# The low rank term's second product: from 32-row float32 tiles to one 128-row float32r product

## Chip, cores and metric

One core of one Trainium2 chip runs the whole kernel. The metric is the device time of one execution in microseconds (us). All arrays are float32 in memory; the kernel's large products run in float32r, on operands that were first split into a rounded high part and a low part that holds the rest.

## The reference, cut to what matters

```python
x = attention(q, k, v)                 # windowed, 4 batches x 8 heads, 576 tokens, 64 wide
xt = x.transpose(0, 2, 1)              # [4, 512, 576]
h = xt @ U @ V                         # U [576, 32], V [32, 576]: the low rank term
u = x + h.transpose(0, 2, 1)
x = u + relu(u @ w_ch1) @ w_ch2        # 512 -> 2048 -> 512
...                                    
```

A gated block with LayerNorm and a 576x576 spatial product follows and gives the output [4, 576, 512]; the change does not touch it. The term in question is small: per batch `xt @ U` gives a [512, 32] matrix, which is then multiplied by V.

## The kernel before, in words

The kernel does not call the engines directly. Every piece of work is handed to a planner (class `Plan`) by `P.add(engine, cost, emit, r=..., w=..., prio=...)`, with a cost in us, the buffers that it reads and writes, and a priority. The planner places the tasks engine by engine in eight passes of a list schedule and emits the instructions in that order, so a change in a few tasks can reorder all the others. Some tasks may go to one of two engines: a PSUM copy by `copy(engines("t", ...))` to ACT (line 416) or DVE (line 417), the scaling of the attention weights to POOL (line 1080) or DVE (line 1082), a `minus` to DVE (line 602) or POOL (line 603).

The first 190 us are the attention. Its work runs over 4 batches x 4 pairs of heads: scores on PE (line 1044), bias and row maximum on DVE (line 1055), exponent on ACT (line 1060), scaling (1080, 1082), transposes on PE (line 1090), the product with v (line 1128). Between these, PE does the first products of the hidden layer for the batches that are done (lines 545 to 547 and 584 to 586, each three matmuls of 128x512: a "trio" below). After each batch come the tokens' transposes (line 1155) and the low rank term:

- `mix` (line 1171): for each pair of heads, U as a 32-column stationary operand against the transposed x, five chunks, float32. The four pairs write the four strips of 32 partitions of one PSUM tile `t`. Batch 0 does it in two halves of two pairs each, the other batches in one.
- One ACT copy of `t` to the SBUF tile `th` (line 416, `th<-at`).
- `up` (line 1184), for each half of 288 tokens: one float32 matmul for each pair, whose contraction is over the pair's own strip of 32 rows, with `th` as stationary and `v32` (V, copied four times, once onto each strip) as moving operand. All products of a half are one task and take as many PSUM buffers at once. A float32 product has two records in the trace.
- An add on DVE for each product into the attention's output `u` (line 1189).

`low_rank_weights` loads U and V, decodes them on ACT and DVE (lines 452 to 465), and copies V from `v4` to the strips of `v32` by four DMAs (line 983). SP issues all DMAs in the planner's order, one behind another, and an issue that waits for its data holds those behind it. PSUM buffers come from the rings `sc` and `at` (three each, four in batch 0).

Of the kernel before, what the change touches and what calls it, by code (L numbers as in the profile page):

```python
# [338 lines left out]
def tile_kernel(ctx, tc, qT, kT, v, U, V, w1, w2, w_in, wspT, bsp, w_out, bias, out):  # L339
    nc = tc.nc  # L340
# [82 lines left out]
    def engines(kind, usual):  # L423
        return BOTH if kind in K["flex"] else (usual,)
# [512 lines left out]
    def constant(name, shape, dtype):  # L937
        return Ring(in_att, name, 1).new(shape, dtype)
# [25 lines left out]
    for p in ps:  # L964
        for t in (0, 8):
            P.add("POOL", 0.1, lambda p=p, t=t: nc.gpsimd.memset(p[:, REST[t] * 128 + 64 : REST[t] * 128 + 128], 0.0),
                  w=[p.part("zero")], prio=-1)
    r_xt, r_th = Ring(in_att, "xt", 2), Ring(in_att, "th", 2)


    u32 = constant("u32", [128, 5, RANK], F32)
    v32 = constant("v32", [128, S], F32)

    def low_rank_weights(prio, early, prio_v, early_v):
        single(u32, [(0, block(U, 0, 128, 0, RANK)), (1, block(U, 64, S, 0, RANK, 4))], 5, RANK, prio, None, early)
        P.add("DVE", 0.1, lambda: nc.vector.memset(u32[64:, 0], 0.0), w=[u32], prio=prio)
        n = S // 2
        v4 = constant("v4", [128, 1, n], F32)
        single(v4, [(0, block(V, 0, RANK, i // 2 * n, i // 2 * n + n), slice(RANK * i, RANK * i + RANK)) for i in range(4)],
               1, n, prio_v, None, early_v)  # L980
        for q in range(2):
            for d in range(2):
                P.dma(64, n, lambda q=q, d=d: nc.sync.dma_start(
                    out=v32[64 * d : 64 * d + 64, q * n : q * n + n], in_=v4[64 * q : 64 * q + 64, 0]),
                    r=[v4], w=[v32.part((q, d))], prio=K["vc"])

    vl = {}
    spare = r_f1.new([128, 128], F32)
# [173 lines left out]
    def low_rank(b, xts, pairs, p0):  # L1162

        sc, tp = (r_sc0, r_at0) if b == 0 else (r_sc, r_at)
        rows = slice(pairs[0] * 32, pairs[-1] * 32 + 32)
        t, th = tp.new([128, 128], F32), r_th.new([128, 128], F32)

        def mix():
            for c in range(5):
                for pair in pairs:  # L1170
                    nc.tensor.matmul(t[pair * 32 : pair * 32 + 32], u32[:, c], xts[pair // 2][:, c, pair % 2],
                                     start=c == 0, stop=c == 4, skip_group_check=True)

        P.add("PE", 5 * 4 * 128 / 2400 + 0.1, mix, r=[u32] + [xts[h].part(c) for h in {p // 2 for p in pairs} for c in (0, 2, 4)],
              w=[t], prio=p0, mode="quarters")
        copy(engines("t", "ACT"), 128, lambda: th[rows], lambda: t[rows], PSUM, r=[t], w=[th], prio=p0 + 0.05)
        for s0 in (0, 288):
            sl = slice(s0, s0 + 288)
            outs = [(sc, tp)[pair % 2].new([128, 288], F32) for pair in pairs]

            def up(sl=sl, outs=outs):
                for pair, o in zip(pairs, outs):
                    d = slice(pair * 32, pair * 32 + 32)
                    nc.tensor.matmul(o.ap(), th[d], v32[d, sl], start=True, stop=True)

            P.add("PE", 4 * 288 / 2400 + 0.1, up, r=[th] + list(v32.parts.values()), w=outs, prio=p0 + 0.1, mode="quarter rows")
            for pair, o in zip(pairs, outs):
                ub = u[b][pair]
                P.add("DVE", dve(288), lambda o=o, ub=ub, sl=sl: nc.vector.tensor_tensor(
                    out=ub[:, sl], in0=o.ap(), in1=ub[:, sl], op=ALU.add),  # L1190
                    r=[o], w=[ub.part(0), ub.part(1), ub], prio=p0 + 0.2)
# [544 lines left out]
```

## Time and profile before

| | us |
|---|---|
| median of the three runs | 714.19 |
| the runs | 713.57, 714.19, 2403.31 |
| the profiled execution, its own time | 713.79 |
| its span, first to last instruction | 712.0 |
| mean granted TensorE clock, of full speed | 1.000 |

The span is the time between the first and the last instruction; 1.8 us of the execution lie outside it. Busy time of an engine is the time in which at least one of its instructions ran. PE's matmuls overlap, so their starts tell more than their durations: the distance from one start to the next is what one of them costs in a full queue.

### The profile page before, as it was taken

How to read it: one execution, taken by the hardware profiler on the slowest of the kernel's cores; microseconds unless marked ns; L12 is line 12 of the kernel's file. 1: busy time of each engine (PE TensorE's matmuls, PEld its weight loads, DVE VectorE, ACT ScalarE, POOL GpSimd, SP SyncE). 2: the span in 40 equal slices, each digit the busy share in tenths (PEclk: the TensorE clock that was granted, in tenths of full speed). 3: DMA queues.
4: the chain of work that ended last, by engine and by line, in shares of the span. 5: the costliest groups of instructions: out<-in, count | busy, mean ns of one | idle time of the engine just before them, and what ended most of it. 6: DMA issues, size and time to landing. Idle time of an engine off the chain costs nothing.

```text
span 712.0 us, 14829 instructions
## 1 busy us (share of the span) xinstructions
PE 701.7 (99%) x5434; PEld 637.8 (90%) x5434; DVE 576.0 (81%) x1637; ACT 394.0 (55%) x1082; POOL 75.0 (11%) x114
## 2 busy tenths in 40 slices
PE   8989999999999999999999999999999999999998
PEld 6767778778799999999999999999998898898896
DVE  6999996775597999999695998696589989859561
ACT  7878666564353655547253562544267566566352
POOL 2243330310400000000000000040010100100000
DMA  8865212210074166628475555447694202100102
GB/s 233 280 221 161 66 52 82 72 53 2 1 225 157 42 228 220 223 106 267 149 225 175 168 195 185 144 148 264 239 386 174 80 30 68 54 22 0 60 1 75
DMA packets 58799, 98.48 MB, mean 138 GB/s; under 512 B 8357, under 2 KB 38309, under 8 KB 58726
## 3 DMA queue, kind: packets, MB, share of 16 engines
q1 hardware_dynamic: 58437, 97.23, 41.2%
q8 instruction: 43, 0.70, 0.4%
q14 instruction: 31, 0.25, 0.1%
q10 hardware_dynamic: 288, 0.30, 0.1%
HBM read 67.67 MB, written 29.54 MB: 137 GB/s over the span
## 4 chain that ended last, share of the span: by engine, by line
PE 88%; DVE 7%; ACT 2%; DMA 1%; issue 1%; POOL 0%; SPq 0%; POOLq 0%; ACTq 0%
PE sc L586 8%; PE sc L584 8%; PE sc L585 8%; PE at L885 6%; PE at L886 6%; PE at L887 6%; PE at L1128 3%; PE sc L1044 2%; PE sc L1423 2%; PE sc L1421 2%; PE sc L1422 2%; PE at L1090 2%; PE at L1423 2%; PE at L1421 2%; PE at L1422 2%; PE acc L584 2%
## 5 line engine op out<-in xcount | busy, mean ns | idle before, releaser
L584 PE MATMUL sc<-h,wa 128*128 128x384 f32 (+1 forms) x328 | 110.6, 337 | 0.0
L585 PE MATMUL sc<-h,wa 128*128 128x384 f32 (+1 forms) x328 | 110.5, 337 | 0.0
L586 PE MATMUL sc<-hl,wa 128*128 128x384 f32 x320 | 108.7, 340 | 0.0
L1060 ACT ACTIVATE p<-p,nmax 128x192 f32<-128x192 f32 (+2 forms) x144 | 61.5, 431 | 10.2 <-DVE nmax L1055 10.0
L584 PEld LDWEIGHTS sc<-h,wa 128*128 128x128 f32 x328 | 61.6, 188 | 0.3
L585 PEld LDWEIGHTS sc<-h,wa 128*128 128x128 f32 x328 | 61.5, 187 | 0.3
L933 DVE TENSOR_TENSOR y<-sc,y 128x384 f32<-128x384 f32 (+1 forms) x96 | 40.7, 450 | 25.6 <-PE sc L586 25.3
L885 PE MATMUL at<-xd,wa 128*128 128x384 f32 x180 | 60.9, 338 | 0.0
L886 PE MATMUL at<-xd,wa 128*128 128x384 f32 x180 | 60.8, 338 | 0.0
L887 PE MATMUL at<-xd,wa 128*128 128x384 f32 x180 | 60.8, 338 | 0.0
L586 PEld LDWEIGHTS sc<-hl,wa 128*128 128x128 f32 x320 | 60.1, 188 | 0.0
L1055 DVE CUSTOM_DVE_ANT_0 p<-sc,bias 128x192 f32<-128x192 f32 (+2 forms) x144 | 40.3, 328 | 12.7 <-PE sc L1044 12.4
L905 ACT COPY c<-at 128x384 f32<-128x384 f32 x54 | 25.8, 478 | 39.2 <-PE at L887 38.9
L416 ACT CAST wa<-st 128x256 fp32r<-128x256 f32 (+1 forms) x62 | 28.1, 475 | 25.2 <-DVE st L465 13.1
L897 ACT ACTIVATE h<-c 128x384 fp32r<-128x384 f32 x54 | 28.4, 526 | 19.7 <-DVE c L892 19.5
L892 DVE TENSOR_TENSOR c<-at,c 128x384 f32<-128x384 f32 x54 | 29.8, 551 | 8.2 <-PE at L887 4.9
L885 PEld LDWEIGHTS at<-xd,wa 128*128 128x128 f32 x180 | 33.8, 188 | 0.0
L886 PEld LDWEIGHTS at<-xd,wa 128*128 128x128 f32 x180 | 33.8, 188 | 0.0
L887 PEld LDWEIGHTS at<-xd,wa 128*128 128x128 f32 x180 | 33.8, 188 | 0.0
L1044 PE MATMUL sc<-kr,qr 64*64 64x192 f32 (+2 forms) x576 | 31.7, 319 | 1.2 <-DMA qr<-in_qT 0.7
L1090 PE MATMUL at<-ident,p 128*128 128x128 f32 x208 | 31.1, 281 | 1.5 <-DVE p L1082 1.4
L1090 PEld LDWEIGHTS at<-ident,p 128*128 128x128 f32 x208 | 23.0, 140 | 10.4 <-issue 3.3
(407 smaller groups left out, 2007.7 us busy)
## 6 DMA issues: line engine op xcount, KB each, us to landing
wa<-in_w SPq DMA_DIRECT2D x32, 512.0 KB, 4.3
xd<-formsa SPq DMA_DIRECT2D x24, 192.0 KB, 3.0
qr<-in_qT SPq DMA_DIRECT2D x15, 288.0 KB, 3.3
kr<-in_kT SPq DMA_DIRECT2D x15, 288.0 KB, 4.0
vr<-in_v SPq DMA_DIRECT2D x16, 256.0 KB, 4.3
raw<-in_w_in SPq DMA_DIRECT2D x8, 512.0 KB, 3.9
kepts<-raw SPq DMA_DIRECT2D x14, 288.0 KB, 2.1
out<-h SPq DMA_DIRECT2D x15, 256.0 KB, 2.0
```

The costliest lines, as they stand in the source:

```text
L584: nc.tensor.matmul(o, wt[:, 0, 0, c], hh[:, j], start=i == 0 and x == 0, stop=False, skip_group_check=True)
L585: nc.tensor.matmul(o, wt[:, 1, 0, c], hh[:, j], start=False, stop=False, skip_group_check=True)
L586: nc.tensor.matmul(o, wt[:, 0, 0, c], hl[:, j], start=False, stop=i == len(wts) - 1, skip_group_check=True)
L885: nc.tensor.matmul(o.ap(), wh()[:, k], xh.ap(), start=start and k == 0, stop=False, skip_group_check=True)
L886: nc.tensor.matmul(o.ap(), wl()[:, k], xh.ap(), start=False, stop=False, skip_group_check=True)
L887: nc.tensor.matmul(o.ap(), wh()[:, k], xl.ap(), start=False, stop=k == 1, skip_group_check=True)
L892: P.add("DVE", dve(N3), lambda: nc.vector.tensor_tensor(out=out.ap(), in0=ps_.ap(), in1=sb.ap(), op=ALU.add), r=[ps_, sb], w=[out], prio=0)
L933: P.add("DVE", dve(m), lambda acc=acc, dst=dst, s=s, m=m, o=o: nc.vector.tensor_tensor(out=dst[:, s : s + m], in0=acc[:, 0, o : o + m], in ...
L1044: nc.tensor.matmul(s[o : o + 64, c0 : c0 + k1 - k0], qr[d, 64 * t : 64 * t + 64], kr[d, k0:k1], start=True, stop=True, skip_group_check=True)
L1055: nc.vector.tensor_tensor_reduce(out=o(), in0=s[:, c0 : c0 + nk], in1=bias_t[:, pair, t % 2, 192 - nk :], scale=-0.125, scalar=BIG, op0=AL ...
L1060: nc.scalar.activation(out=o(), in_=o(), func=AF.Exp, scale=-1.0, bias=nmax[:, sl, t : t + 1], accum_out=sums[:, sl, t : t + 1])
L1090: P.add("PE", 0.109, lambda pt=pt, n_=n_, s0=s0: nc.tensor.transpose(pt[:, n_ - s0], p[:, n_ * 128 : n_ * 128 + 128], ident), r=[p.part(t) ...
```

## The change

The 32-row products become products over all 128 rows, in float32r. For each pair a zeroed tile `four[:, pair]` takes, on strips of 32 rows, the high part of `t`, its low part, and the high part again; the fourth strip stays zero. `v32` takes V's high part on the strips that stand against the first two and V's low part on the others. One product then sums high x high, low x high and high x low. (For pairs 2 and 3, whose strips of `t` are the lower ones, the strips are placed the other way round.) Each product is a task of its own with one PSUM buffer. `t` to `four` takes three operations for each pair: a copy (ACT or DVE), a subtraction (DVE), a copy (ACT or DVE). V gets a copy (ACT) and a subtraction (DVE) more before its four DMAs, and POOL a memset of `four` at the start.

```diff
-    r_xt, r_th = Ring(in_att, "xt", 2), Ring(in_att, "th", 2)
+    r_xt, four = Ring(in_att, "xt", 2), constant("four", [128, 4, 128], F32R)
+    P.add("POOL", 0.3, lambda: nc.gpsimd.memset(f32(four.ap()), 0.0), w=[four.part(pair) for pair in range(4)], prio=-1)
...
-    v32 = constant("v32", [128, S], F32)
+    v32 = constant("v32", [128, S], F32R)
...
-        v4 = constant("v4", [128, 1, n], F32)
+        v4, v4h = constant("v4", [128, 1, n], F32), Ring(in_left, "y", 0, more=["y_4"]).new([128, n], F32R)
...
+        P.add("ACT", act(n, 0.09), lambda: nc.scalar.copy(out=v4h.ap(), in_=v4[:, 0]), r=[v4], w=[v4h], prio=K["vc"])
+        minus(("DVE",), n, lambda: v4[:, 0].bitcast(F32R), lambda: v4[:, 0], lambda: f32(v4h.ap()), r=[v4h], w=[v4], prio=K["vc"])
         for q in range(2):
-            for d in range(2):
-                P.dma(64, n, lambda q=q, d=d: nc.sync.dma_start(
-                    out=v32[64 * d : 64 * d + 64, q * n : q * n + n], in_=v4[64 * q : 64 * q + 64, 0]),
-                    r=[v4], w=[v32.part((q, d))], prio=K["vc"])
+            for d, (src, t) in enumerate(((lambda: f32(v4h.ap()), v4h), (lambda: v4[:, 0], v4))):
+                P.dma(64, n, lambda q=q, d=d, src=src: nc.sync.dma_start(
+                    out=f32(v32[64 * d : 64 * d + 64, q * n : q * n + n]), in_=src()[64 * q : 64 * q + 64]),
+                    r=[t], w=[v32.part((q, d))], prio=K["vc"])
...
-        copy(engines("t", "ACT"), 128, lambda: th[rows], lambda: t[rows], PSUM, r=[t], w=[th], prio=p0 + 0.05)
+        strip = lambda g: slice(32 * g, 32 * g + 32)
+        for pair in pairs:
+            part, low = four.part(pair), 0 if pair == 1 else 1
+            copy(engines("t", "ACT"), 128, lambda pair=pair: four[strip(pair), pair], lambda pair=pair: t[strip(pair)], PSUM, r=[t], w=[part], prio=p0 + 0.05)
+            P.add("DVE", dve(128), lambda pair=pair, low=low: nc.vector.tensor_tensor(
+                out=four[strip(low), pair], in0=t[strip(pair)], in1=f32(four[strip(pair), pair]), op=ALU.subtract), r=[t], w=[part], prio=p0 + 0.05)
+            copy(engines("t", "ACT"), 128, lambda pair=pair: four[strip(2 if pair < 2 else 0), pair], lambda pair=pair: t[strip(pair)], PSUM, r=[t], w=[part], prio=p0 + 0.05)
         for s0 in (0, 288):
             sl = slice(s0, s0 + 288)
-            outs = [(sc, tp)[pair % 2].new([128, 288], F32) for pair in pairs]
-
-            def up(sl=sl, outs=outs):
-                for pair, o in zip(pairs, outs):
-                    d = slice(pair * 32, pair * 32 + 32)
-                    nc.tensor.matmul(o.ap(), th[d], v32[d, sl], start=True, stop=True)
-
-            P.add("PE", 4 * 288 / 2400 + 0.1, up, r=[th] + list(v32.parts.values()), w=outs, prio=p0 + 0.1, mode="quarter rows")
-            for pair, o in zip(pairs, outs):
-                ub = u[b][pair]
+            for pair in pairs:
+                o, ub = (sc, tp)[pair % 2].new([128, 288], F32), u[b][pair]
+                P.add("PE", mm(288), lambda pair=pair, o=o, sl=sl: nc.tensor.matmul(o.ap(), four[:, pair], v32[:, sl], start=True, stop=True),
+                      r=[four.part(pair)] + list(v32.parts.values()), w=[o], prio=p0 + 0.1)
```

In the order of instructions, 32 products stand in place of 32; 16 subtractions and 18 of the 32 copies are on DVE, 14 copies on ACT, where 5 copies (`th`) were. Of the scalings of attention weights DVE has 81 in place of 87, and of its other copies out of PSUM (line 417) 47 in place of 52. Lines of the attention have a number two or three higher in the changed kernel.

The first place is PE at the low rank term of the last batch (`xt` transposed x, `u_419` and `u_443` U, `v_441` and `v_471` the tile v32). Before:

```order
L1171 MATMUL at<-xt,u_419 32x128 x20
L584 MATMUL acc<-h,wa 128x512
L585 MATMUL acc<-h,wa 128x512
L586 MATMUL acc<-h,wa 128x512
L1184 MATMUL sc<-v_441,th 128x288
L1184 MATMUL at<-v_441,th 128x288
L1184 MATMUL sc<-v_441,th 128x288
L1184 MATMUL at<-v_441,th 128x288
L584 MATMUL acc<-h,wa 128x512
```

In the changed kernel the same place on PE reads:

```order
L1173 MATMUL at<-xt,u_443 32x128 x20
L584 MATMUL acc<-h,wa 128x512
L585 MATMUL acc<-h,wa 128x512
L586 MATMUL acc<-h,wa 128x512
L1189 MATMUL sc<-v_471,four 128x288 x2
L1189 MATMUL at<-v_471,four 128x288
L1189 MATMUL sc<-v_471,four 128x288
L1189 MATMUL at<-v_471,four 128x288 x2
L584 MATMUL acc<-h,wa 128x512
```

One trio stands between `mix` and the first products in both; behind it six products follow in place of four, and the last two stand two trios later.

The second place is DVE in the last batch, from the transposed tokens to the adds. Before, nothing of the low rank term stood between them:

```order
L417 COPY u<-at 128x4x64
L417 COPY xt<-at 128x512
L552 SCALAR_TENSOR_TENSOR h<-f_2822,h 128x512
L594 TENSOR_TENSOR y<-acc,u 128x128
L594 TENSOR_TENSOR y<-acc,u 128x384
L1189 TENSOR_TENSOR u<-sc,u 128x288
```

In the changed kernel DVE has there:

```order
L417 COPY u<-at 128x4x64
L417 COPY xt<-at 128x512
L552 SCALAR_TENSOR_TENSOR h<-f_2839,h 128x512
L417 CAST four<-at 32x128 x2
L1182 TENSOR_TENSOR four<-at,four 32x128 x2
L417 CAST four<-at 32x128 x2
L1182 TENSOR_TENSOR four<-at,four 32x128 x2
L594 TENSOR_TENSOR y<-acc,u 128x128
```

Eight operations on strips were put in, four more copies to `four` are on ACT.

The third place is DVE in the second half of batch 0 (`st` weights that are decoded, `p_77` attention weights). Before:

```order
L417 COPY xt<-at 128x512
L1068 RECIPROCAL rinv<-rinv 128x9
L458 TENSOR_SCALAR st<-st 128x512
L1082 TENSOR_SCALAR p_77<-p_77,rinv 128x192 x4
L1082 TENSOR_SCALAR p_77<-p_77,rinv 128x64
L1082 TENSOR_SCALAR p_77<-p_77,rinv 128x192 x3
L1082 TENSOR_SCALAR p_77<-p_77,rinv 128x128
L459 TENSOR_SCALAR st<-st 128x512
L1189 TENSOR_TENSOR u<-sc,u 128x288
```

In the changed kernel:

```order
L417 COPY xt<-at 128x512
L462 SCALAR_TENSOR_TENSOR st<-wa,st 128x512
L1085 TENSOR_SCALAR p_77<-p_77,rinv 128x192
L1085 TENSOR_SCALAR p_77<-p_77,rinv 128x64
L1085 TENSOR_SCALAR p_77<-p_77,rinv 128x192 x2
L1085 TENSOR_SCALAR p_77<-p_77,rinv 128x128
L1085 TENSOR_SCALAR p_77<-p_77,rinv 128x192
L1182 TENSOR_TENSOR four<-at,four 32x128 x2
L417 CAST four<-at 32x128 x2
L465 SCALAR_TENSOR_TENSOR st<-wa,st 128x512
L1191 TENSOR_TENSOR u<-sc,u 128x288
```

Three of the nine scalings left DVE for POOL, and two subtractions and two copies came in.

## Rows read from the trace of the kernel before

**Rows 1.** The page: busy time by engine, and the chain by engine
```profile
PE 701.7 (99%) x5434; PEld 637.8 (90%) x5434; DVE 576.0 (81%) x1637; ACT 394.0 (55%) x1082; POOL 75.0 (11%) x114
...
PE 88%; DVE 7%; ACT 2%; DMA 1%; issue 1%; POOL 0%; SPq 0%; POOLq 0%; ACTq 0%
```

**Rows 2.** Busy time in stretches of the attention
```profile
core 0: us, PE busy (x) PEld busy (x) DVE busy (x) ACT busy (x) POOL busy (x), PEclk, DMA share, GB/s
...
20.00:50.00 30.00, 27.26 (x446) 19.87 (x440) 28.90 (x113) 23.65 (x80) 11.05 (x9) 1.00 0.75 245
50.00:80.00 30.00, 29.01 (x341) 22.16 (x339) 30.00 (x107) 24.73 (x85) 12.80 (x20) 1.00 0.50 146
...
107.00:186.00 79.00, 78.76 (x1012) 60.82 (x1011) 51.97 (x206) 42.53 (x148) 11.04 (x18) 1.00 0.15 47
```

**Rows 3.** The chain that ended last, around 80 us (start, us, what)
```profile
79.36 0.61 DVE y L594
80.02 0.50 PE acc L584
```

**Rows 4.** Timeline of PE, low rank term of the last batch (start, us, instruction)
```profile
179.56 1.30 PE L1171 MATMUL at<-xt,u 128*32 128x128 f32 x40
...
182.69 0.47 PE L584 MATMUL acc<-h,wa 128*128 128x512 f32 x1 [0.24 <-PE at L1184]
183.00 0.40 PE L585 MATMUL acc<-h,wa 128*128 128x512 f32 x1
183.23 0.40 PE L586 MATMUL acc<-h,wa 128*128 128x512 f32 x1
183.56 0.51 PE L1184 MATMUL sc<-v,th 32*128 32x288 f32 x1
...
184.59 0.39 PE L585 MATMUL acc<-h,wa 128*128 128x512 f32 x1
```

**Rows 5.** Timeline of PE, first half of batch 0
```profile
30.50 0.51 PE L1184 MATMUL sc<-v,th 32*128 32x288 f32 x1
...
31.67 0.87 PE L1090 MATMUL at<-ident,p 128*128 128x128 f32 x6
```

**Rows 6.** Timeline of PE, float32r products of 128 rows and 288 columns
```profile
537.28 0.29 PE L1574 MATMUL at<-wf,x 128*128 128x288 f32 x1
...
538.48 0.29 PE L1576 MATMUL sc<-wf,x 128*128 128x288 f32 x1
```

**Rows 7.** Groups by shape on DVE: mean ns of one behind the comma
```profile
L594 DVE TENSOR_TENSOR y<-sc,u 128x128 f32<-128x128 f32 x2 | 0.6, 292 | 3.9 <-PE sc L586 3.9
```

**Rows 8.** Timeline of DVE: neighbours on all partitions, then one on a strip
```profile
546.34 0.45 DVE L1601 SCALAR_TENSOR_TENSOR y<-y 128x288 f32<-128x288 f32 x1
546.70 0.45 DVE L1593 TENSOR_TENSOR y<-f,y 128x288 f32<-128x288 f32 x1
...
684.85 0.46 DVE L1601 SCALAR_TENSOR_TENSOR y<-y 128x288 f32<-128x288 f32 x1
685.34 0.42 DVE L602 TENSOR_TENSOR ve<-h,ve 32x256 fp32r<-32x256 f32 x1
```

**Rows 9.** Timeline of ACT, the copy behind the last batch's mix
```profile
180.93 0.27 ACT L416 COPY th<-at 128x128 f32<-128x128 f32 x1 [1.34 <-PE at L1171]
```

**Rows 10.** Timeline of DVE and PE, second half of batch 0
```profile
39.64 3.06 DVE L1082 TENSOR_SCALAR p<-p,rinv 128x192 f32<-128x192 f32 x9
...
41.48 0.44 PE L1090 MATMUL at<-ident,p 128*128 128x128 f32 x2 [0.99 <-DVE p L1082]
```

**Rows 11.** U's last decoding step on DVE; landing of V's DMAs (line 983)
```profile
25.83 0.32 DVE L465 SCALAR_TENSOR_TENSOR u<-raw,u 128x160 uint32<-128x160 uint32 x1
...
DMA to landing us min/median/max: 2.0/2.1/4.8
```

**Rows 12.** Timeline of POOL, a memset at the start
```profile
0.87 0.15 POOL L966 MEMSET p<- 128x64 f32 x1
```

**Rows 13.** Timeline of PE, first product that needs the last batch's u
```profile
191.88 0.34 PE L545 MATMUL at<-xd,wa 128*128 128x384 f32 x1
```

More of the change, by code (lines that the diff above doesn't have):

```diff
@@ L1164, in low_rank @@
         sc, tp = (r_sc0, r_at0) if b == 0 else (r_sc, r_at)
-        rows = slice(pairs[0] * 32, pairs[-1] * 32 + 32)
-        t, th = tp.new([128, 128], F32), r_th.new([128, 128], F32)
+        t = tp.new([128, 128], F32)
         def mix():
```

## The prediction, made before the changed kernel ran

> **What bounds the kernel now.** I read the page first, then busy time by stretches, then the chain of waits, and last the timelines around the low rank term. The page says that PE is busy for 701.7 of 712.0 us and that 88% of the chain that ended last are PE, 7% DVE [rows 1]. So work taken from PE counts, unless another engine leads just there. The stretches show where that is: from 20 to 50 us DVE is busy for 28.90 of 30 us and PE for 27.26, from 50 to 80 us DVE has no idle time at all, and from 107 to 186 us PE has 78.76 of 79 and DVE only 51.97 [rows 2]. The chain agrees: it runs on DVE until the add at 79.36, and from 80.02 on PE [rows 3]. Batch 0's low rank term (two halves, at 30 and 42 us) thus lies where DVE leads, those of batches 1, 2 and 3 behind 80 us, where PE leads. After 186 us the change touches nothing.
>
> **PE: what goes.** In the last batch the second half's four products stand between a trio and the next. Starts in a full queue are 0.23 apart (183.00 to 183.23). The place behind the trio is therefore free at 183.46; the first product starts at 183.56, and the second matmul of the next trio at 184.59, so that the trio's place began at 184.36 [rows 4]. Four packed products hold PE for 184.36 - 183.46 = 0.90 us. Batches 1 to 3 have six such groups: 6 x 0.90 = 5.4. A float32r product of 128 rows and 288 columns takes, from start to start, (538.48 - 537.28) / 9 = 0.133 [rows 6]; 24 of them take 3.2. PE saves 2.2 us there. In batch 0 each half has two groups of two products, from 30.50 to 31.67, 1.17 us [rows 5], and then 4 x 0.133 = 0.53; twice the difference is 1.3. Together 3.5 us.
>
> About 0.2 of each group's 0.90 are the gaps of 0.10 ahead of it and behind it [rows 4]. The Trainium skill (TensorEngine Tiling (Array Packing), Key Properties) says that a change of tiling mode drains the engine; the trace agrees. The same page (Performance Considerations, When to Use Tiling) gives 32-row contractions fourfold row tiling, and that speaks against this change. What that rule leaves out here is that the packed product is float32, with two records for each product, while the full one is float32r with one; it is the third rival below.
>
> **DVE and ACT: what comes.** DVE gets 16 subtractions and 18 copies, all 128 columns from PSUM. The trace has no such operation on a strip; the nearest is the add of 128x128 out of PSUM, 0.292 [rows 7]. I take 0.30 for each. From below: neighbours on all partitions overlap, a start is 0.36 behind the last although each lasts 0.45 [rows 8], so 0.29 - 0.09 = 0.20 is the least; from above 0.42, what an operation on 32 partitions with 256 columns lasts [rows 8]. So 34 x 0.30 = 10.2 us in the whole attention, of which batch 0 has 8 operations (2.4), and V's subtraction of 288 columns as long as its like, 0.45 [rows 8]. Three of the nine scalings in batch 0's second half leave DVE, 3 x 3.06 / 9 = 1.0 [rows 10].
>
> The operation on the strip started at 685.34, after its predecessor's end at 684.85 + 0.46, without overlap [rows 8]. The Trainium skill (VectorE: DVE Perf Modes, Two Vector instructions with no wait between them) has the rule for it: an instruction whose operand begins in another group of 32 partitions than the one before is held until the earlier ones are finished. By it nearly every new operation pays its full length, and the cost is nearer 0.30 than 0.20; without it the sum would be 6.8 instead of 10.2 us.
>
> ACT gets 14 copies for 5, 0.27 each [rows 9], and one of V: under 3 us, for an engine with 6 us idle in 20 to 50 us and more than 36 in 107 to 186 us [rows 2]. Cost nothing; the cover goes only where a product waits for a copy, and that is counted next. The memset of `four` on POOL has eight times the columns of one that lasts 0.15 [rows 12], so at most 1.2 us; it stands among the constants at the start, and POOL is busy for 11% [rows 1]. Cost nothing.
>
> V's low part now waits for a subtraction that stands behind U's last decoding on DVE (25.83 before [rows 11]). SP waits with it and holds the loads of v, weights and q behind. It would end near 26.6; with 2.0 to 4.8 to land [rows 11] the strips are there between 28.6 and 31.4, and the first product, at 30.50 before [rows 5], moves back with its own operands. Taken as nothing; at worst it costs 0.9.
>
> **The step from mix to the products.** Before, one ACT copy, 0.07 behind the end of `mix` (180.86) and 0.27 long [rows 4, 9], and a trio (0.69) hid it. Now a pair needs copy, subtraction, copy, and the four pairs queue on DVE. In the last batch DVE does eight in a row: 0.07 + 8 x 0.30 + a hand-over of 0.07 and the last ACT copy of 0.27 = 2.8 us from the end of `mix` until the last pair is ready. PE has one trio and four or five products before that, 1.2 to 1.4 us, then the waiting product holds the trios behind it. So PE would stand for up to 1.6; 0.2 an operation would make it 0.8. I take 1.3. In batches 1 and 2 two trios and a third among the products cover 2.3 to 2.5 of 2.8 and 3.4; I take 0.3 and 0.5. The wait of 0.24 behind the first group [rows 4], for the PSUM buffers that a group took all at once, goes. Sum 1.9; the ends are -0.2 (the trios cover everything) and 3.3 (1.6 in the last batch and twice the price in the other two). What is late next: the adds into u, then the hidden layer's products. The first one that needs the last batch starts at 191.88 [rows 13], some 7 us behind that batch's last product, and keeps most of that.
>
> **The sum.** Batch 0, where DVE leads: 2.4 + 0.45 - 1.0 = 1.9 more on DVE, of which its idle 1.1 in 20 to 50 us [rows 2] can take some: 0.8 is left, between 0 and 2.9 (nothing moved away). PE's 1.3 there gives nothing, since PE waits for DVE anyway: 0.99 at 41.48 alone [rows 10]. Batches 1 to 3: -2.2 + 1.9. Together 0.8 - 2.2 + 1.9 = +0.5. The profiled execution would go from 713.79 to 714.3. It lies 0.4 under the median of the runs, 714.19, so the median becomes 714.7: no change.
>
> **Rivals.**
> First, the whole saving on PE counts. For it: 88% of the chain are PE, and with fillers from 50 us on PE never stands long. Against it: DVE without idle time up to 80 us. With no new wait and the old one gone, -3.5 - 0.2: 710.5.
>
> Second, slower: DVE leads through batches 0 and 1, and everything it gets there lands on the chain. Its place is 20 to 107 us, where the batch's chain of exponent, scaling, transpose hangs on DVE. Price: 16 x 0.30 + 0.45 - 1.0 = 4.2; batches 2 and 3 save 4 x (0.90 - 0.53) = 1.5 and wait 0.5 + 1.3 - 0.24 = 1.6; sum +4.3: 718.5. It decides as soon as DVE's net addition ahead of 107 us exceeds what idle time and the moved scalings take away, 1.1 + 1.0. For it: 30.00 of 30 [rows 2]. Against it: ACT and POOL are idle for a good part of the same stretch, and work that can go either way was moved to them.
>
> Third, the packing was worth its mode: a full product takes as long as a whole packed group without its gaps, 0.70. Then a group becomes 2.8 and the six cost 11.4 more: 726. The row of a full float32r product, 0.133 [rows 6], excludes nearly all of it.
>
> Fourth, the change of order. The planner moves hundreds of other instructions on every engine and SP; that may shift the rest by a few us either way, and no row prices it.
>
> **How the numbers follow.** The forecast (713 to 716.5) has 0.50, the first rival 0.24, the second 0.18, the third 0.01, the fourth, where it outweighs the others, 0.07. The range takes the first two rivals' prices and a little more: 710.0 to 719.5; the forecast's own is 713 to 716.5. About 2%, 14 us, is what a measurement of this kernel can tell from no change; none of the priced cases but the third reaches it. Faster by more 0.02, within 0.95, slower by more 0.03.
>
> **What would show it.** Right: products of the new line 0.13 apart with no gap ahead of them; PE standing for about 1 us behind `mix` in the last batch, released by ACT or DVE on `four`; DVE still leading the chain up to 80 us; strip operations that start only behind their predecessor's end. Wrong: PE idle behind `mix` in no batch (then the first rival), DVE without idle time up to 107 us and PE's idle time there up by several us (the second), starts of the new products well over 0.13 apart (the third), or a difference that sits after 190 us (the fourth).

## The result, and the profile after

The changed kernel takes 722.72 us (median of five, 722.33 to 726.05) where 714.19 stood: a ratio of 1.0131 of the means (the run of 2403.31 left out), 95% interval 1.0103 to 1.0159. That is slower, by less than 2%, and outside the range of 710.0 to 719.5. The ratio and interval behind each later time are taken against runs of the kernel before that were made beside it.

The page of after, busy time and chain by engine [rows 1], and the first two stretches of [rows 2]:

```profile
PE 707.6 (98%) x5402; PEld 645.1 (89%) x5402; DVE 582.9 (81%) x1662; ACT 397.2 (55%) x1097; POOL 76.5 (11%) x120
...
PE 91%; DVE 7%; ACT 1%; issue 0%; DMA 0%; DVEq 0%
```

```profile
20.00:50.00 30.00, 25.07 (x395) 18.33 (x394) 29.47 (x107) 23.89 (x83) 11.07 (x10) 0.96 0.80 249
50.00:80.00 30.00, 28.14 (x324) 21.57 (x321) 26.84 (x99) 22.96 (x76) 12.98 (x15) 0.93 0.41 122
```

PE is busy for 5.9 us more, although it has less to do. The column behind POOL says why: the granted clock, 1.00 in every stretch of [rows 2], is 0.96 and 0.93 here. Three short stretches make that, each behind a wait of PE (1.21 us until 47.20, 1.70 until 60.84, 1.30 and 0.45 until 193.26); there the clock is at its lower level, 1.2 of 2.4 GHz, or near it:

```profile
48.00:50.00 2.00, 2.00 (x16) 1.66 (x17) 1.82 (x6) 1.64 (x4) 1.17 (x1) 0.50 0.27 94
62.00:64.00 2.00, 2.00 (x6) 1.61 (x5) 1.27 (x6) 1.54 (x8) 0.56 (x1) 0.50 0.00 0
196.00:198.00 2.00, 2.00 (x7) 1.66 (x7) 0.82 (x2) 1.04 (x5) 0.61 (x2) 0.56 0.00 0
```

The group of the new products says what PE waited for in the first and the third of these waits: DVE's copies into `four`, 3.8 us in the whole attention. The second wait was for DVE's step on the hidden layer's `h` (line 552), which is no strip step.

```profile
L1189 PE MATMUL sc<-v,four 128*128 128x288 f32 x16 | 4.6, 340 | 4.3 <-DVE four L417 3.8 <-ACT four L416 0.5
```

This profiled execution was the longest of the five (726.05). A repeat of the same kernel gave 722.3 (1.0111, 1.0090 to 1.0132) and a profile of 722.08, near the median; I take lengths from that one. In the repeat the clock fell only behind the third wait, and PE is busy for 702.9 us. Its first two waits are about as long as in the profile of 726.05 (1.21 until 45.63 and 1.75 until 58.33), and the clock stayed at 1.00 behind them:

```profile
56.00:58.00 2.00, 0.58 (x8) 0.20 (x2) 2.00 (x4) 0.29 (x1) 2.00 (x3) 1.00 0.71 202
58.00:60.00 2.00, 1.67 (x7) 1.41 (x8) 2.00 (x14) 1.88 (x9) 2.00 (x2) 1.00 0.23 78
...
190.00:192.00 2.00, 2.00 (x7) 1.58 (x6) 1.88 (x6) 0.00 (x0) 0.00 (x0) 0.55 0.00 0
192.00:194.00 2.00, 2.00 (x8) 1.67 (x7) 0.82 (x2) 0.93 (x4) 0.50 (x1) 0.60 0.00 0
```

PE's timeline gives the starts of `mix` in batches 1, 2 and 3 and of the first product of the next stage, which needs the last batch ([rows 13] before). Behind it nothing differs: up to the first product of the stage after that, before and after both take 32.65 us (224.53 and 236.63).

| profile of | mix of batch 1 | to batch 2 | to batch 3 | to next stage | next stage starts |
|---|---|---|---|---|---|
| before | 86.11 | 46.70 | 46.75 | 12.32 | 191.88 |
| after, 726.05 | 93.90 | 47.20 | 47.42 | 15.46 | 203.98 |
| after, repeat | 89.84 | 47.20 | 47.48 | 15.45 | 199.97 |
| no low part | 89.46 | 45.49 | 45.87 | 12.02 | 192.84 |
| low part in batch 0 alone | 89.94 | 45.50 | 45.88 | 12.02 | 193.34 |
| after with fillers | 90.23 | 47.20 | 47.48 | 13.87 | 198.78 |
| `t` copied to SBUF first | 92.61 | 46.18 | 46.83 | 13.38 | 199.00 |
| changed in batch 0 alone | 92.00 | 47.70 | 47.28 | 11.39 | 198.37 |

The rows from the fourth on are runs of the section on the experiments.

The repeat loses 3.73 us up to batch 1's mix, 0.50 and 0.73 in the next two batches and 3.13 in the last: 8.09.

The last batch in the repeat, PE, then DVE, then ACT (start, us, instruction, idle time ahead and its releaser) [rows 4, 9]:

```profile
184.52 1.30 PE L1173 MATMUL at<-xt,u 128*32 128x128 f32 x40
...
186.33 0.40 PE L586 MATMUL acc<-h,wa 128*128 128x512 f32 x1
188.03 0.54 PE L1189 MATMUL sc<-v,four 128*128 128x288 f32 x2 [1.30 <-DVE four L417]
188.43 0.37 PE L1189 MATMUL at<-v,four 128*128 128x288 f32 x1
189.25 0.40 PE L1189 MATMUL sc<-v,four 128*128 128x288 f32 x1 [0.45 <-ACT four L416]
189.54 0.54 PE L1189 MATMUL at<-v,four 128*128 128x288 f32 x2
189.91 0.40 PE L584 MATMUL acc<-h,wa 128*128 128x512 f32 x1
```

```profile
186.18 0.28 DVE L417 CAST four<-at 32x128 fp32r<-32x128 f32 x1 [2.31 <-ACT four L416]
186.78 0.29 DVE L417 CAST four<-at 32x128 fp32r<-32x128 f32 x1 [0.33 <-ACT four L416]
187.10 0.57 DVE L1182 TENSOR_TENSOR four<-at,four 32x128 fp32r<-32x128 f32 x2
187.69 0.60 DVE L417 CAST four<-at 32x128 fp32r<-32x128 f32 x2
188.32 0.59 DVE L1182 TENSOR_TENSOR four<-at,four 32x128 fp32r<-32x128 f32 x2
```

```profile
185.89 0.26 ACT L416 CAST four<-at 32x128 fp32r<-32x128 f32 x1 [2.01 <-PE at L1173]
186.49 0.26 ACT L416 CAST four<-at 32x128 fp32r<-32x128 f32 x1 [0.35 <-DVE four L417]
188.94 0.54 ACT L416 CAST four<-at 32x128 fp32r<-32x128 f32 x2 [2.19 <-DVE four L1182]
```

Read the three together: 185.89 ACT, 186.18 DVE, 186.49 ACT, 186.78 DVE, then six on DVE, then two on ACT. Twelve steps in one row, never two at once, although each pair has its own strip of `t` and its own part of `four`: 185.89 to 189.48, 0.30 a step. And they run kind by kind, all four first copies ahead of everything else, so that the first pair is ready only after the seventh (at 187.97; PE's first product starts at 188.03) and the second after the eighth.

In batches 1 and 2 of the repeat PE stands in the same way, for less:

```profile
92.36 0.39 PE L586 MATMUL acc<-h,wa 128*128 128x512 f32 x1
93.42 0.37 PE L1189 MATMUL sc<-v,four 128*128 128x288 f32 x1 [0.67 <-DVE four L417]
...
94.17 0.39 PE L584 MATMUL acc<-h,wa 128*128 128x512 f32 x1
...
139.53 0.40 PE L586 MATMUL acc<-h,wa 128*128 128x512 f32 x1
140.54 0.53 PE L1189 MATMUL sc<-v,four 128*128 128x288 f32 x2 [0.62 <-DVE four L417]
...
141.16 0.39 PE L584 MATMUL acc<-h,wa 128*128 128x512 f32 x1
```

Counted by starts, as the prediction counts (a trio's next place is 0.23 behind its last start, a product takes 0.133), PE loses 189.91 - 186.56 - 6 x 0.133 = 2.55 in the last batch, 94.17 - 92.59 - 2 x 0.133 = 1.31 in batch 1, and 141.16 - 139.76 - 3 x 0.133 = 1.00 in batch 2, each around the first group of products.

Batch 0 shows in DVE's share from 15 us to batch 1's mix. In the profile of before it is busy for 69.22 of 71.11 us there (first line); in the repeat (second line)

```profile
15.00:86.11 71.11, 67.27 (x959) 50.48 (x959) 69.22 (x253) 55.95 (x192) 26.20 (x31) 1.00 0.61 193
15.00:89.84 74.84, 67.37 (x975) 51.08 (x968) 72.99 (x266) 59.49 (x202) 29.73 (x35) 1.00 0.59 179
```

for 3.77 us more, in a stretch that is 3.73 longer. DVE leads there from end to end, and its idle time (1.89, now 1.85) took nothing; PE's idle time went from 3.84 to 7.47. The groups of the repeat in this stretch price what is new:

```profile
L417 DVE CAST four<-at 32x128 fp32r<-32x128 f32 x4 | 1.1, 286 | 0.1
L1182 DVE TENSOR_TENSOR four<-at,four 32x128 fp32r<-32x128 f32 x4 | 1.1, 286 | 0.1
...
L602 DVE TENSOR_TENSOR v<-v,y 128x288 fp32r<-128x288 f32 x1 | 0.5, 461 | 0.0
```

2.7 us are new operations; the other 1.1 is the balance of work of before that the planner moved, over that point or to another engine (for instance, 20 decoding steps of lines 462 and 465 stand ahead of it where 18 did, and 49 bias steps of 128x192 where 45 did, but 22 scalings of 128x192 for 27).

### The profile page after: what moved, and what is told of

Its sections match the earlier page's. It is cut to its first block, busy times and chain, and to the rows that moved or that the text cites. A ratio compares the mean times of both kernels' runs of the same rounds, so it can differ in the third digit from the quotient of the medians.

```text
span 724.1 us, 14834 instructions
## 1 busy us (share of the span) xinstructions
PE 707.6 (98%) x5402; PEld 645.1 (89%) x5402; DVE 582.9 (81%) x1662; ACT 397.2 (55%) x1097; POOL 76.5 (11%) x120
## 4 chain that ended last, share of the span: by engine, by line
PE 91%; DVE 7%; ACT 1%; issue 0%; DMA 0%; DVEq 0%
PE sc L586 8%; PE sc L584 8%; PE sc L585 8%; PE at L885 6%; PE at L886 6%; PE at L887 6%; PE sc L1047 3%; PE at L1131 3%; PE at L1093 3%; PE sc L1425 2%; PE sc L1424 2%; PE sc L1423 2%; PE at L1423 2%; PE at L1425 2%; PE at L1424 2%; PE f L545 2%
## 5 line engine op out<-in xcount | busy, mean ns | idle before, releaser
L1047 PE MATMUL sc<-kr,qr 64*64 64x192 f32 (+2 forms) x576 | 34.2, 334 | 0.4 <-DMA kr<-in_kT 0.4
L1504 ACT CAST x<-h 128x256 fp32r<-128x256 f32 x56 | 21.9, 406 | 18.2 <-DVE h L1467 13.5
```

The source lines that it names most:

```text
L1047: nc.tensor.matmul(s[o : o + 64, c0 : c0 + k1 - k0], qr[d, 64 * t : 64 * t + 64], kr[d, k0:k1], start=True, stop=True, skip_group_check=True)
```

## The experiments

Theory 1: PE stands because `t` gets into `four` through a row of strip steps in which the two engines take turns, and the clock falls behind the standing. Theory 2: V's split and the longer hold of SP in batch 0. Theory 3: the planner's new order alone. Where a run keeps "its own order", steps left out are still planned, but nothing is issued for them.

**Low parts left out**

In place of the subtraction and of the second copy:

```diff
+            P.add("DVE", dve(128), lambda: None, r=[t], w=[part], prio=p0 + 0.05)
+            P.either([("ACT", act(128), lambda: None), ("DVE", dve(128), lambda: None)], r=[t], w=[part], prio=p0 + 0.05)
```

> The changed kernel in its own order, with the low part left out: of the three strip steps of each pair only the first copy is made, the subtraction and the second copy are not (so the low rank term is computed from rounded products alone). Theory 1 (PE stands because the strips of t reach four through a chain in which ScalarE and VectorE take turns, and the granted clock falls behind the standing): each chain has 2 or 4 steps instead of 6 or 12, the wait from the mix to the first product falls in batch 3 from 3.5 us to under 1.5 us, the half-clock stretch behind it goes, and the time is 715 to 717 us. Theory 2 (V's split and the longer hold of SP's queue in batch 0): nothing that it names is taken away, 721 to 723. Theory 3 (the new order of the work alone): the order is the same, 721 to 723.

714.94 (1.0007, 0.9997 to 1.0017), just under what theory 1 expected. The same order without the low part gives back nearly the whole loss (7.8 of 8.5). It still has the wait of 1.70 for line 552, and in its profile the clock fell behind that wait (0.50 from 58 to 60), so that wait is not what the loss hangs on. PE's timeline of this run, last batch:

```profile
182.63 0.40 PE L586 MATMUL acc<-h,wa 128*128 128x512 f32 x1
182.86 0.47 PE L1188 MATMUL sc<-v,four 128*128 128x288 f32 x2
```

The first product follows the trio at the trio's own pace, 0.23, with no gap, and batches 1 to 3 are 46.70 + 46.75 + 12.32 - 45.49 - 45.87 - 12.02 = 2.4 us shorter than before.

The same in batches 1 to 3 alone:

```diff
+            if b > 0:
+                P.add("DVE", dve(128), lambda: None, r=[t], w=[part], prio=p0 + 0.05)
...
+                continue
```

> The changed kernel in its own order, with the low part (subtraction and second copy of each pair) left out in batches 1 to 3 and kept in batch 0, so those batches are computed from rounded t alone. If the loss sits in every batch's chain, as the milestones of the run without any low part say (some 2 us of its 8 in batch 0, 5 in batches 1 to 3): 717 to 718.5 us, batch 1's mix as late as in the changed kernel, and no wait of over 0.3 us at the first product in batches 1 to 3. Rival, the loss is made in batch 0, where VectorE leads, and is only carried on: 720.5 to 722.5 us.

717.52 (1.0044, 1.0029 to 1.0059). So in this order the low part costs 722.7 - 717.5 = 5.2 in batches 1 to 3, and 717.5 - 714.9 = 2.6 in batch 0. Of the 2.6 the clock is a part: the one execution of the five with a mean clock of 0.999 took 715.43 (it is the one in the table, only 0.5 behind the run without low parts, in which the clock fell once), the others, at 0.994 and 0.995, 717.05 to 718.14.

**One copy of `t` into SBUF first**

```diff
+        def once(pair):
+            if not there:
+                nc.scalar.copy(out=th[rows, 4, 0], in_=t[rows])
+                there.append(1)
+            return th[pair * 32 : pair * 32 + 32, 4, 0]
...
-            copy(engines("t", "ACT"), 128, lambda pair=pair: four[strip(pair), pair], lambda pair=pair: t[strip(pair)], PSUM, r=[t], w=[part], prio=p0 + 0.05)
+            copy(engines("t", "ACT"), 128, lambda pair=pair: four[strip(pair), pair], lambda pair=pair: once(pair), PSUM, r=[t], w=[part], prio=p0 + 0.05)
```

(`th` is a part of `xt` that `mix` has read; the other two steps likewise.)

> The changed kernel in its own order, with one more step: ScalarE first copies t from PSUM into SBUF once, and all strip steps read that copy instead of t. Theory 1, in the form that the two engines take turns because both read the same PSUM bank: the copy costs 0.25 to 0.3 us per group, the turns go, the wait from the mix to the first product falls in batch 3 from 3.5 us to about 2 us and the time is 716 to 719 us. Theory 1 in the form that the number of strip steps alone makes the chain long: the copy is added to it, 722 to 724. Theory 2 (V's split) and theory 3 (the order): 722 to 723.

721.16 (1.0098, 1.0083 to 1.0113), between the two expectations of theory 1. DVE and ACT of this run in the last batch:

```profile
187.34 0.46 DVE L417 CAST four<-xt 32x128 fp32r<-32x128 f32 x2 [2.37 <-ACT xt L1173]
187.83 0.57 DVE L1189 TENSOR_TENSOR four<-xt,four 32x128 fp32r<-32x128 f32 x2
...
188.92 0.60 DVE L1189 TENSOR_TENSOR four<-xt,four 32x128 fp32r<-32x128 f32 x2
```

```profile
187.04 0.27 ACT L1173 COPY xt<-at 128x128 f32<-128x128 f32 x1 [2.06 <-PE at L1180]
187.34 1.26 ACT L416 CAST four<-xt 32x128 fp32r<-32x128 f32 x4
```

With its source in SBUF the same work runs on both engines at once, from 187.04 to 189.52 with the added copy: 2.5 us in place of 3.6. So the turns came from reading one PSUM tile, and taking them away is worth 1.6 of the 8.5. The table shows where the rest sits in this run: batches 1 to 3 take 46.18 + 46.83 + 13.38 = 106.4, 3.7 less than in the repeat and 0.6 more than before, but batch 1's `mix` comes at 92.61, 6.5 later than before, and in batch 0 the clock fell twice. The Trainium skill (PSUM — Partial Sum Buffer, PSUM bank collisions raise a hardware error) says that two engines must not use one bank in the same 32 partitions at once, and may in different ones. The strips lie in different ones; the waits here are semaphores of the program, and no run shows what the chip would do without them.

**V's split**

```diff
-        P.add("ACT", act(n, 0.09), lambda: nc.scalar.copy(out=v4h.ap(), in_=v4[:, 0]), r=[v4], w=[v4h], prio=K["vc"])
-        minus(("DVE",), n, lambda: v4[:, 0].bitcast(F32R), lambda: v4[:, 0], lambda: f32(v4h.ap()), r=[v4h], w=[v4], prio=K["vc"])
+        P.add("ACT", act(n, 0.09), lambda: None, r=[v4], w=[v4h], prio=K["vc"])
+        P.add("DVE", dve(n), lambda: None, r=[v4h], w=[v4], port=True, prio=K["vc"])
...
```

All four transfers then carry V itself.

> The changed kernel in its own order, with V's split left out: V's rounded copy and its subtraction are not made, and all four transfers copy V itself (so the low part of V is V again). Theory 2 (V's split, and the time that its transfers and what stands behind them on SP's queue wait for it): the first mix of batch 0 comes 1 to 1.6 us earlier, the first hidden product at 49 to 51 us instead of 54.7, and the time is 718 to 721 us. Theory 1 (the chains of strip steps) and theory 3 (the order): 722 to 723, with the waits behind the mixes as they were.

722.87 (1.0123, 1.0108 to 1.0138). The other way round, the kernel before with the copy and the subtraction added, and its transfers waiting for them:

> The kernel before, with V's rounded copy on ScalarE and its subtraction on VectorE added, and V's transfers waiting for them; the subtraction's result, which the products here would not use as a value of V, is taken in V's place (so the low rank term is computed from V's low part alone). Theory 2 (V's split): 716 to 718 us, the first hidden product 1.5 to 4 us later than at 48.8. Theory 1 (the chains of strip steps): 714 to 715. Theory 3 (the order): the planner lays the batches out anew here too, so anything from 711 to 719 with no wait at the mix.

714.99 (1.0015, 1.0003 to 1.0027). Theory 2 falls: V's split costs nothing in the one and under a microsecond in the other.

**PE's waits filled**

```diff
+    FILL = {(0, 2, 0): 5, (3, 0, 0): 5, (3, 2, 0): 2}
...
+                    for _ in range(fill):
+                        nc.tensor.matmul(o[:, :128], hot.ap(), hot.ap(), start=True, stop=True)
                     nc.tensor.matmul(o.ap(), four[:, pair], v32[:, sl], start=True, stop=True)
```

> The changed kernel with products that nobody reads put into three of PE's waits: five of 128 columns before the first product of batch 0's second group and of batch 3, two before the third pair of batch 3, some 0.21 us each, written to a part of the output tile that the product after them overwrites. Nothing becomes ready earlier. If the granted clock falls because PE stood there (two stretches, some 1.7 us lost in each): the stretches at 48 to 51 us and 194 to 198 us stay at the full clock and the time is 719 to 720.5 us. Rival, the clock falls for another reason or costs nothing on the path: 722 to 723.5.

720.84 (1.0092, 1.0076 to 1.0109). The last batch of this run, PE (two records for each of the five), and the stretch behind it; the repeat of after has 0.55 in the same stretch (above):

```profile
186.96 1.28 PE L1194 MATMUL sc<-hot 128*128 128x128 f32 x10
188.42 0.54 PE L1195 MATMUL sc<-v,four 128*128 128x288 f32 x2 [0.18 <-DVE four L417]
```

```profile
190.00:192.00 2.00, 2.00 (x12) 1.74 (x12) 2.00 (x7) 0.00 (x0) 0.00 (x0) 1.00 0.00 0
```

All four runs had a mean clock of 1.000, and work that nobody reads made the kernel 1.5 to 1.9 us faster. The last batch went from 15.45 to 13.87. That is the clock's share: of the nine executions of after only one, of the repeat, kept 1.000, and it took 721.05; the two of the repeat at 0.995 took 722.52 and 723.86. The wait of 1.72 for line 552 was not filled, and the clock stayed at 1.00 behind it, as in the repeat.

**The planner's numbers.** First the turns told to it:

```diff
+            part, low, turn = four.part(pair), 0 if pair == 1 else 1, t.part("turn")
...
-            copy(engines("t", "ACT"), 128, lambda pair=pair: four[strip(pair), pair], lambda pair=pair: t[strip(pair)], PSUM, r=[t], w=[part], prio=p0 + 0.05)
+            copy(engines("t", "ACT"), 200, lambda pair=pair: four[strip(pair), pair], lambda pair=pair: t[strip(pair)], PSUM, r=[t], w=[part, turn], prio=p0 + 0.05)
```

> The changed kernel with the planner told what the strip steps are: each takes turns with the others that read the same t, at 0.27 us on VectorE and 0.23 on ScalarE in place of 0.20 and 0.17. The work is the same, the order is made anew. If PE stands only because the planner puts the products too early: it puts two or three more hidden products between mix and first product, the waits of 0.6 to 1.3 us in batches 1 to 3 and the clock behind them go, 716 to 719 us. Rival, the steps themselves hold VectorE in batch 0 and ScalarE's and VectorE's other work everywhere: 720.5 to 724.

719.76 (1.0082, 1.0066 to 1.0097), between the two expectations. Then a higher cost alone (160 in place of 128):

> The changed kernel with the planner's cost of each strip step raised a little (0.19 us on ScalarE and 0.23 on VectorE, in place of 0.17 and 0.20), nothing else: the same instructions in a new order. If the loss is that of the steps in batch 0, with the waits of this kernel's order on top: 718 to 722 us, no order of it near 714. Rival, the loss is that of one unlucky order: within 2 us of 714.2.

719.35 (1.0067, 1.0045 to 1.0088). And the same nudge on the one copy of the kernel before (200 in place of 128):

> The kernel before with one number of the planner changed: the copy of t is costed at 0.23 us on ScalarE and 0.27 on VectorE in place of 0.17 and 0.20. The instructions are the same, their order is made anew. What it measures is how far the order alone moves this kernel. If the order of batch 0 is a matter of a few us (theory 3): a median 1.5 us or more away from 714.2, on either side. Rival, the order alone moves nothing that matters and batch 0's loss belongs to the new steps: within 1 us of 714.2.

713.24, no difference (0.9998, 0.9986 to 1.0009). The three orders of the changed kernel spread over 3 us and none comes near 714; the two of before stay within one. Theory 3 explains up to 3 of 8.5, and the clock is in that figure: the nudged kernel stood at 0.999 and 1.000 in all four executions, and against the one of the repeat that kept 1.000 (721.05) it is 1.7 faster. The repeat:

> The changed kernel itself, once more, beside the others on the same chip. Nothing is changed: 722 to 723.5 us, a span of 719 to 722, and three stretches of about half the granted clock (behind the waits at 47, 60 and 192 us), with V's first product less late than in the profiled execution of 726 us.

722.3; the clock fell in one stretch of its profile, not in three.

**Where it is made.** The change in batches 1 to 3 alone, with batch 0 as before on V as it came:

```diff
+        if b == 0:
+            th = r_t0.new([128, 128], F32)
+            copy(engines("t", "ACT"), 128, lambda: th[rows], lambda: t[rows], PSUM, r=[t], w=[th], prio=p0 + 0.05)
...
+                        nc.tensor.matmul(o.ap(), th[d], v32f[d, sl], start=True, stop=True)
...
+            return
```

> The change in batches 1 to 3 alone: batch 0 has the products of the kernel before, on V as it came, and V's split follows behind them for the later batches. If batch 0's part of the loss (some 3.5 us up to batch 1's mix) comes from the strips and V's split there: batch 1's mix at 85.5 to 87 us, the later batches as in the changed kernel with its waits (0.7 us visible, 1.7 in length, in each), 717 to 719 us. Rival, the planner's new order in batch 0 is what costs, whatever the steps are: it is new here again, and batch 1's mix comes at 88 to 91 us, 719.5 to 722.

714.66, no difference (1.0008, 0.9999 to 1.0017), and below both expectations; batch 1's `mix` starts at 83.02. In the last batch the twelve steps still run in one row, 178.17 to 181.83, but six trios stand between `mix` and the products, which wait for nothing:

```profile
182.03 0.39 PE L586 MATMUL acc<-h,wa 128*128 128x512 f32 x1
182.25 0.42 PE L1217 MATMUL sc<-v,four 128*128 128x288 f32 x2
182.52 0.29 PE L1217 MATMUL at<-v,four 128*128 128x288 f32 x1
182.65 0.30 PE L1217 MATMUL sc<-v,four 128*128 128x288 f32 x1
182.78 0.29 PE L1217 MATMUL at<-v,four 128*128 128x288 f32 x1
182.92 0.39 PE L584 MATMUL acc<-h,wa 128*128 128x512 f32 x1
```

And in batch 0 alone (`if b > 0:` in the same place):

> The change in batch 0 alone: V's split and the strips serve batch 0, and batches 1 to 3 have the products of the kernel before on V as it came. If the loss is made where VectorE leads and nothing covers the chain: batch 1's mix at 89 to 92 us, a stretch of half clock between 44 and 52 us, 717.5 to 720.5 us. Rival, it is the chains in batches 1 to 3 that cost: 714 to 716. Rival, order alone: anything from 712.5 to 717.

721.49 (1.0098, 1.0078 to 1.0118), a microsecond over its range. Here batch 1's mix starts at 92.00, and PE's second half of batch 0 and the stretch behind it read

```profile
42.81 0.50 PE L1215 MATMUL at<-y 128*128 128x288 f32 x2 [1.71 <-DVE y L417]
...
45.08 1.43 PE L1053 MATMUL sc<-kr,qr 64*64 64x64 f32 x17 [1.45 <-DVE u L1217]
```

```profile
46.00:48.00 2.00, 2.00 (x22) 1.13 (x18) 1.30 (x10) 0.84 (x5) 2.00 (x2) 0.50 0.12 38
```

(`four` lies in `y` here.) From 15 us to 92.00 DVE is busy for 72.44 of 77.00 us: 3.2 more than before, and idle for 2.7 more, so in this order a part of batch 0's loss is DVE's work and a part its waiting. Changed in batch 0 alone, in an order of its own, the kernel has nearly the whole loss; in batches 1 to 3 alone the planner found cover for the chains. The 5.2 that they cost in the order of after is therefore not a price of the steps but of that order: the parts do not add. With the turns told to the planner as well, the change in batches 1 to 3:

> The change in batches 1 to 3 alone (714.7 us), with the planner told that the strip steps of one t take turns, at 0.27 and 0.23 us. TensorE has 2.4 us less work in these batches (by the run with no low parts), so if the planner now covers every chain with hidden products: 712 to 713.5 us, faster than the kernel before by a little. Rival, the order it makes gives the gain back in batch 0 or VectorE's extra steps hold it: 714 to 716.

714.35 (1.0005, 0.9994 to 1.0016): covered but for one wait of 0.95 for `four` in batch 1, and still no gain.

**A third form without strips**

```diff
+        copy(engines("t", "ACT"), 128, lambda: th[rows], lambda: t[rows], PSUM, r=[t], w=[th], prio=p0 + 0.05)
+        P.add("DVE", dve(128), lambda: nc.vector.tensor_tensor(
+            out=tl[rows], in0=t[rows], in1=f32(th[rows]), op=ALU.subtract), r=[t, th], w=[tl], prio=p0 + 0.05)
...
+                for i, (c, v) in enumerate(((th, v32), (th, v32l), (tl, v32))):
+                    for pair, o in zip(pairs, outs):
+                        d = slice(pair * 32, pair * 32 + 32)
+                        nc.tensor.matmul(o.ap(), c[d], v[d, sl], start=i == 0, stop=i == 2)
```

> A third form of the low rank term: the same split of t and V, but no strips. ScalarE rounds all rows of t in one step, VectorE subtracts in one step, and the second product is three float32r products of 32 rows per pair and half (rounded by rounded, rounded by V's low part, t's low part by rounded), the pairs beside each other on the 32-row quarters as before. V's two parts lie in two tiles, so V takes eight transfers in place of four. If the strip chain is the loss: two steps per group instead of 6 or 12, no wait of over 0.8 us at the first product, each group of eight or four products shorter than the 0.90 us of before, and 711 to 714 us, faster than both kernels. Rival, V's split and the new order in batch 0 cost by themselves: 715 to 718. Rival, products of 32 rows gain nothing from float32r: 714 to 716.

717.81 (1.0056, 1.0042 to 1.0069). With right costs and the rounding on ACT alone:

> The third form in all batches, with the two steps costed at what they take (0.23 and 0.27 us) and the rounding on ScalarE alone. In the run without these costs the waits of 0.5 to 1.3 us in batch 0 were followed by 7 us at about half the granted clock, some 3.4 us lost. If the order with right costs has no such waits: 711.5 to 714 us. Rival, batch 0's VectorE is so full that some order of waits comes back: 715 to 719.

716.57 (1.0038, 1.0025 to 1.0050). In batches 1 to 3 alone:

> The third form (three float32r products of 32 rows, two steps per group) in batches 1 to 3, and batch 0 as in the kernel before. From the third form's own milestones: batches 1 to 3 take 104.7 us from mix to the next stage in place of 105.8, so if batch 0 stays as before, 711.5 to 713.5 us, faster than the kernel before by 1 to 2 us. Rival, the new order in batch 0 costs again: 715 to 719.

720.16 (1.0074, 1.0059 to 1.0088), a miss: the planner put V's split into batch 0, and PE had two half-clock stretches there. The last two put the split behind batch 0:

> The third form in batches 1 to 3, batch 0 as in the kernel before, and V's split made to wait for batch 0's last product, so that nothing new stands in batch 0. If batch 0 then takes what it takes before (batch 1's mix at 84 to 87 us, or a waiting planner's equivalent) and the later batches keep their 103.3 us to the next stage: 711 to 713 us, faster than the kernel before by 1 to 3. Rival, the saving is given back in waits for VectorE whatever the form, as in the runs of the strips in batches 1 to 3: 714 to 716.

715.98 (1.0026, 1.0017 to 1.0035).

> The same with the two steps costed at what they take (0.23 us on ScalarE, 0.27 on VectorE) and the rounding on ScalarE alone: another order of the same work. If the saving is real and only the order decides how much of it stays: 711 to 714, and within 2 us of the run beside it. Rival: 714 to 717.

713.58 (0.9990, 0.9979 to 1.0000), the best of these, and not to be told from before, though in its profile the clock fell in batch 0 too. No form beat the kernel before by more than its spread.

## Why the prediction was wrong

- **PE's saving** was right: 2.2 us forecast in batches 1 to 3, 2.4 measured where no low part stands in the way. Where `four` is ready the new products stand 0.13 apart without a gap, as forecast (182.52 to 182.78 in the change in batches 1 to 3 alone); the third rival is out.
- **The prices** were right: 0.28 to 0.29 for a strip step on DVE (0.30 forecast), 0.26 on ACT, 0.46 for V's subtraction; the memset took 0.52 at the start. A strip step on DVE starts only behind its predecessor's end, as forecast. V's way over SP was taken as nothing; V's whole split cost nothing in the changed kernel and 0.8 in the one before.
- **"The step from mix to the products" failed.** It let ACT's copies run beside DVE, took eight steps in a row, and reckoned the last pair ready 2.8 us behind `mix`, with waits of 0.3, 0.5 and 1.3 in batches 1, 2 and 3 (1.9 with the old wait gone). The trace shows one row over both engines, 3.6 us, the first pair ready only after seven steps, and PE loses 1.3, 1.0 and 2.6 around its first products. Against the run without low parts, batches 1 to 3 are 110.13 - 103.38 = 6.7 us longer; 1.6 of it is the clock (15.45 against 13.87). Two sums of this step don't come out by its own figures: batch 2's 3.4 less a cover of at most 2.5 is 0.9, not 0.5, and the upper end is 1.6 + 1.6 - 0.24 = 3.0, not 3.3; neither would have moved the forecast by more than 0.4.
- **"Batch 0" failed:** 0.8 forecast, since DVE's idle 1.1 us and three moved scalings were to take 2.1 of its 2.9. DVE's idle time stayed and its busy time rose by 3.8. Fewer scalings do stand there (27 for 33, 10.5 us for 11.7), but other work came in their place. This was the second rival's place and mechanism, at 4.2 on DVE, and PE's idle time there rose by 3.6, the sign that the prediction named for it; its 718.5 is still 4 us short, since it priced the waits of the later batches as the forecast did, and the clock not at all. The third rival's 726 lies nearer only by chance.
- **The clock** was in no term: 1.5 to 1.9 us in the typical run, more in the longest.
- **The change of order** was given 0.07 as a case of its own; its spread, up to 3 us with the clock in it, is nearly as large as the forecast's own range.

What stays open: how much of batch 0's loss is the new steps alone. Every kernel that changes them also has a new order, and the run in its own order (2.6 for the low part) still had the rounded copies, V's split and that order. And why batches 1 to 3 gain nothing from 2.4 us less on PE: in the change in batches 1 to 3 alone PE is busy for 171.39 of the 177 us from 15 to 192 (before 172.92), and the rest went into new waits for DVE and ACT elsewhere (0.61 for `h` and 0.56 for `u` around 136, for instance), which were not taken away.

## What to carry to other kernels

A saving on one engine that is paid for with many small steps on two others is kept only where other work covers those steps: find the stage where nothing covers them (here the first batch) and leave the old form there; here that took the loss away, and won nothing. Count a chain of steps that read one PSUM tile as one row over all the engines that take part, and look in which order its parts come out. Where an order comes from a planner, nudge one of its numbers on both kernels before believing a difference of a few microseconds.

## What the runs showed of the hardware that was not expected

A wait of 1 to 2 us of TensorE can be followed by 3 to 4 us at about half the granted clock, and that can cost as much again as the wait: in the repeat PE waited 1.30 and 0.45 us up to 189.25, the clock is 0.55 from 190 to 192 and 0.60 from 192 to 194, and filling this wait with idle products kept 1.00 and took 1.58 us off the batch. It does not have to be: waits of 1.21 and 1.75 in batch 0 of the same execution were followed by 1.00, while waits of 1.21 and 1.70 at the same places were followed by 0.50 in the profile of 726.05. What decides it no run here shows.

Products of 32 rows in float32r run beside each other on the quarters as the float32 ones do. In the third form the twelve of a half start within 0.4 us (PE, the run in batches 1 to 3, three of them):

```profile
189.74 0.40 PE L1219 MATMUL sc<-v,th 32*128 32x288 f32 x1
...
189.98 0.29 PE L1219 MATMUL sc<-v32l,th 32*128 32x288 f32 x1
...
190.12 0.29 PE L1219 MATMUL sc<-v,tl 32*128 32x288 f32 x1
```

Between the trios around them they hold PE for (190.68 - 0.23) - (189.42 + 0.23) = 0.80 us, where four float32 ones held it for 0.90 [rows 4] and four full products take 4 x 0.133 = 0.53 from start to start.
